# Two neighbouring PSUM banks for every step that takes two, in a kernel whose order a planner makes

## The chip, the core and the metric

The kernel runs on one core of a Trainium2 chip. The metric is the time of one execution in microseconds, as the device counts it; the number to predict is the median of several executions. The core has five engines with a queue each: TensorE (PE in the profile, with its weight loads shown apart as PEld), VectorE (DVE), ScalarE (ACT), GpSimd (POOL) and SyncE (SP, which here issues DMAs). Every queue is worked off in the order in which the program wrote it. An instruction that depends on another engine's work waits at a semaphore, and everything behind it in its own queue waits with it. PE leaves its results in PSUM, 128 partitions of eight banks with 512 f32 values each; VectorE and ScalarE read them there.

## What is computed

Two stages follow each other. The first is a Nystrom attention over 8 batches, 8 heads, 576 positions and a head size of 64, with 32 landmarks: three softmaxes, a pseudo-inverse by six iterations, and a product of four factors.

```
A = sm(q, k_lm);  Bm = sm(q_lm, k_lm);  C = sm(q_lm, k)     # k_lm, q_lm: means of 18 positions
Z = Bm.T / (norm_1(Bm) * norm_inf(Bm) + 1e-06)
for _ in range(6):
    Z = 2 * Z - Z @ Bm @ Z
x = A @ Z @ C @ v
```

The second is a mixture of 8 experts over the 4608 resulting rows of 512 values. Each row goes to the expert with the largest logit, and is scaled by that expert's gate.

```
logits = normalize(x) @ normalize(expert_emb).T / tau
e = argmax(logits);  out = gate[e] * (relu(x @ w1[e]) @ w2[e])       # w1: 512x1024, w2: 1024x512
```

## The kernel before

The kernel guesses one expert for each batch, runs the whole batch through it, and has a general path (the function `general`) for inputs in which a row chose otherwise; on the inputs timed here that path is not taken. f32 factors are split into two f16 parts, so a product takes three f16 matmuls.

Each batch is cut into steps, written as Python generators. `inverse` forms the landmark softmax; `powers` does the six iterations (tile `ek`); `values` is C times v in two halves (tiles `ec`, `ct`, `u`); `queries` is A in two halves (transposed into `ae`, then `ab`); `landmarks` forms the combined factor and the logits' weights (`wgd`); `rows` gives logits and norms in five chunks (its last reader is ScalarE's `junk`, L1134); `first_weights` folds the attention factor into w1 (`ww`), and `first` and `second` are the expert's two layers (`ht`, `yt`). `first` and `second` are the bulk of PE's work. The other steps of the batches to come are woven into it.

What sets the order is the class `Weave`, a planner that runs on the host while the program is written. Each generator yields what it wants next: an engine for so many nanoseconds (`T`, `V`, `A`, `G`), a buffer (`get`), or a flag. The planner keeps a clock for each engine, takes the request that can start first, or among those close to it the one of highest priority, and lets that generator write its instructions. So the instructions of every queue stand in the order in which the planner started them. A buffer carries the planned time at which it came free, and whoever asks gets the ones that have been free longest.

PSUM is one tile `ps` of eight banks (L489). A step calls `take(n)` for one or two banks. Shares limit how many banks a kind of step may hold: 5 for attention steps, 3 for the first layer, 2 for the second. One bank, the highest, is kept for matmuls that only keep the array busy (`keep_warm`, L598) until the first expert layer starts, and joins the others then. Two banks at once are taken by `inverse` (1 time a batch), `values` (4), `queries` (2), `landmarks` (1), `rows` (5) and `first_weights` (4), which is 17 takes for each of eight batches, 136 in all. If the two banks that came free first are x and y, the step's view of them is `ps[:, x:y + 1:y - x]`: a slice that starts at bank x and steps by y - x.

No wait is written by hand. The framework that records the instructions compares what each of them reads and writes and places the semaphore waits. In the built program of this kernel, 282 waits between PE, DVE and ACT join two instructions that have no bank in common, and no other tile either; in each of the 282 one side holds a pair of banks that are apart, and the other side's bank lies between them. The planner knows nothing of such waits.

Of the kernel before, what the change touches and what calls it, by code (L numbers as in the profile page):

```python
# [60 lines left out]
GUESS_LAT = 2500.0  # L61
NBANKS = 8
NSUM = 3

ATT, NPH, NPY = 5, 3, 2

# [41 lines left out]
class Weave:  # L108
# [64 lines left out]
    def tally(self, name, n):  # L173

        self.count[name] += 1
        if self.count[name] == n:
            self.flag(name)

    def _start(self, g, safe=True):
        r, t = g[3], g[1]  # L180
        if r[:2] == ("use", "pe") and safe:
            m = self.margin if g[5] else self.bmargin
            return max(t, g[6] + m, self.free["pe"])
        if r[0] == "use":
            return max(t, self.free[r[1]])
        if r[0] == "sleep":
            return t + r[1]
        if r[0] == "until":
            return max(t, r[1])
        if r[0] == "any":  # L190
            return min(max(t, self.free[o[0]]) for o in r[1])
        if r[0] == "get":
            b, n = self.buffers[r[1]], r[3] if len(r) > 3 else 1
            return max(t, sorted(b)[n - 1][0]) if len(b) >= n else None
        return max(t, self.flags[r[1]]) if r[1] in self.flags else None

    def run(self, *until):

        while self.gens and not (until and all(f in self.flags for f in until)):
            ready = [(self._start(g), g) for g in self.gens]  # L200
            ready = [(t, g) for t, g in ready if t is not None]

            safe = min((t for t, g in ready if g[3][:2] == ("use", "pe")), default=0.0)
            if safe > self.free["pe"]:
                ready = [(min(t, self._start(g, False)) if g[3][:2] == ("use", "pe") else t, g) for t, g in ready]
            assert ready, [g[3] for g in self.gens]
            first, lead = min(ready, key=lambda x: (x[0], x[1][3][0] in ("use", "any")))
            at, best = max(((t, g) for t, g in ready if g[3][:2] == lead[3][:2] and t <= first + SLACK),
                           key=lambda x: (x[1][3][2] if x[1][3][0] == "get" and len(x[1][3]) > 2 and x[1][3][2] is not None else x[1][2], -x[0]))
            r = best[3]  # L210
            if r[0] == "use":

                soon = [(t, g) for t, g in ready if g[2] >= max(AHEAD, best[2] + 100) and g[3][:2] == r[:2] and t < at + r[2] - EPS]
                if soon:
                    at, best = min(soon, key=lambda x: x[0])
                    r = best[3]
            g_t, best[1], best[4] = best[1], at, None
            if r[0] == "any":
                t = g_t
                r = ("use", *min(r[1], key=lambda o: max(t, self.free[o[0]]) + sum(o[1:]))[:2])  # L220
                best[4] = r[1]
                at = max(t, self.free[r[1]])
            if r[:2] == ("use", "pe") and self.warm:
                t = self.free["pe"]
                ns = self.warm((at - t) * (0.5 if self.cold(t) else 1.0) * WARM if at - t > WMIN else 0.0)
                if ns:
                    self.array(t, ns, 2.3 * ns)
                ns = self.warm(self.lacking(at))
                if ns:
                    at = self.array(at, ns, 2.3 * ns)  # L230
            self.last = at
            if r[0] == "use":
                end = self.array(at, r[2], r[4]) if r[1] == "pe" else at + r[2]
                self.free[r[1]] = end
                best[1] = end + (LAT[r[1]] if r[3:4] in ((), (None,)) else r[3])

                best[6] = best[1] if best[1] > end else 0.0
            elif r[0] == "get":
                got = sorted(self.buffers[r[1]])[:r[3] if len(r) > 3 else 1]
                best[6] = max(best[6], got[-1][0])  # L240
                for x in got:
                    self.buffers[r[1]].remove(x)
                best[4] = [i for _, i in got]
            elif r[0] == "wait":
                best[6] = max(best[6], self.flags[r[1]])
            self._step(best)
        self.now = self.last
# [228 lines left out]
def nystrom_moe(ctx: ExitStack, tc: tile.TileContext, qT, kT, v, emb, w1, w2, out):  # L476
# [12 lines left out]
    ps = psum.tile([P, NBANKS, 512], F32, name="ps")  # L489

    def view(ids):

        if len(ids) == 1:
            return ps[:, ids[0]]
        x, y = sorted(ids)
        return ps[:, x:y + 1:y - x]

    def take(n, share="att"):

        yield "get", share, None, n  # L500
        ids = yield "get", "bank", None, n

        def done():
            wv.put("bank", *ids)
            wv.put(share, *ids)

        return view(ids), done
# [158 lines left out]
    def sums(b, nm, src):  # L666
        if b >= NSUM:
            yield "wait", ("a", b - NSUM)
            yield "wait", ("u", b - NSUM)
        sm = sums_of[nm, b] = wk.tile([P, 4, M], F32, name=nm + "sum", bufs=NSUM)  # L670
        half = None
        for x in range(2):
            r = 2 * x
            yield "wait", (nm, b, x)
            if b == 1:
                yield "wait", ("e", 0)
            sv = src[:, r:r + 2].rearrange("p r (m t) -> p (r m) t", t=SEG)
            if (yield "any", (("pool", 1360), ("dve", 1270, SBIAS if b >= SUMS_DVE else -SBIAS))) == "pool":
                yield "get", "half"
                half = wk.tile([P, 2 * M, SEG // 2], F32, name="half", bufs=1)  # L680
                pool.tensor_tensor(out=half, in0=sv[:, :, 0:9], in1=sv[:, :, 9:18], op=ALU.add)  # L681
                yield V(576)
                sv = half
            vec.tensor_reduce(sm[:, r:r + 2].rearrange("p r m -> p (r m)"), sv, axis=AX.X, op=ALU.add)
            if sv is half:
                wv.put("half")
        wv.flag((nm + "s", b))
        wv.tally((nm + "use", b), 3)
# [786 lines left out]
    n = nc.values_load(mi[0:1, 0:1], min_val=0, max_val=NT)  # L1475
# [41 lines left out]
```

## Time and profile before

| | |
|---|---|
| median of three executions | 544.4 us (542.37 to 549.75) |
| the profiled execution, its own time | 546.0 us |
| its span, from the first to the last instruction | 544.3 us |
| mean granted TensorE clock | 0.976 of full speed |
| busy: PE, DVE, ACT, POOL | 459.4, 350.3, 248.3, 81.7 us |
| instructions on PE, DVE, ACT | 5664, 1123, 576 |

Busy time is the time in which an engine had an instruction in work; the rest of the span it stood idle. The view of waits adds up, for pairs of engine and tile, the idle time that ended when the second finished; it says how often this happened and what the longest stop was. The timeline shows instructions in the order of time, with the idle time before each and who ended it in brackets. The windows view gives the busy time of each engine in a stretch of the span, and the clock granted there (PEclk).

### The profile page before, as it was taken

To read this page: it belongs to the slowest core of one execution; us is meant where nothing else is said; L and a number is where in the kernel's file an instruction comes from. 1 tells how busy PE (TensorE), PEld (TensorE's weight loads), DVE (VectorE), ACT (ScalarE), POOL (GpSimd) and SP (SyncE) were. 2 spreads that over 40 slices of the span, in tenths; PEclk is the share of its full clock that TensorE was granted. 3 is DMA by queue.
4 is the path that set the end of the run, shared out by engine and by line. 5 is a ranking of instruction groups with operands and counts; after the bars stand their busy time and mean duration, and the time that the engine had idled before them with its cause. 6 is when DMAs were issued, how large, how long until landed. Compare 5 with 4: busy or idle time off the path is not lost. (4 is left out here: it accounts for less than half of the span.)

```text
span 544.3 us, 13967 instructions
## 1 busy us (share of the span) xinstructions
PE 459.4 (84%) x5664; PEld 251.3 (46%) x5664; DVE 350.3 (64%) x1123; ACT 248.3 (46%) x576; POOL 81.7 (15%) x79
## 2 busy tenths in 40 slices
PE   8797897898787878977999988888878779989994
PEld 3343553435543344532555445543545336635642
DVE  5696794679777675686875728878454766654400
ACT  1266333653466323673358315854157333852410
POOL 2054000023100310233301000322000000010000
PEclk9799898999999998899999999999999999999998
DMA  8693226562159412952258015801172011821011
GB/s 315 236 374 101 88 90 238 162 227 89 45 185 319 160 52 61 375 178 107 85 206 331 35 55 171 325 22 63 60 261 95 20 40 43 308 84 48 3 58 36
DMA packets 29945, 78.22 MB, mean 144 GB/s; under 512 B 2864, under 2 KB 14256, under 8 KB 28080
## 3 DMA queue, kind: packets, MB, share of 16 engines
q1 hardware_dynamic: 29728, 77.15, 39.5%
q8 instruction: 46, 0.75, 0.6%
q14 instruction: 27, 0.22, 0.1%
q10 hardware_dynamic: 144, 0.10, 0.1%
HBM read 61.96 MB, written 15.27 MB: 142 GB/s over the span
## 5 line engine op out<-in xcount | busy, mean ns | idle before, releaser
L510 PE MATMUL ps<-w2c,ht 128*128 128x512 f16 (+1 forms) x1152 | 211.1, 346 | 22.2 <-DVE ww L1297 6.2
L510 PEld LDWEIGHTS <-ht 128*128 128x128 f16 (+1 forms) x1152 | 90.3, 102 | 109.8 <-issue 43.7
L510 PE MATMUL ps<-ab,ww 128*128 128x288 f16 x768 | 112.8, 291 | 15.9 <-DVE ae L872 3.2
L510 PEld LDWEIGHTS <-ww 128*128 128x128 f16 x768 | 71.9, 99 | 50.2 <-issue 26.1
L1343 ACT ACTIVATE ht<-ps 128x288 f16<-128x288 f32 x128 | 51.9, 408 | 57.0 <-PE ps L510 41.7
L1345 DVE SCALAR_TENSOR_TENSOR ht<-ps,ht 128x288 f16<-128x288 f32 x128 | 56.7, 449 | 30.1 <-ACT ht L1343 22.7
L1421 ACT ACTIVATE yt<-ps,gfac 128x512 f32<-128x512 f32 (+1 forms) x34 | 21.8, 642 | 66.7 <-PE ps L510 50.6
L1335 DVE SCALAR_TENSOR_TENSOR w2c<-wstage,wsc,w2c 128x1024 f16<-128x1024 f32 x32 | 41.8, 1307 | 0.2
L1134 ACT ACTIVATE junk<-ps 128x512 bf16<-128x512 f32 (+1 forms) x40 | 23.9, 596 | 38.1 <-PE ps L510 15.3
L1297 DVE SCALAR_TENSOR_TENSOR ww<-ps,wsc,ww 128x512 f16<-128x512 f32 x32 | 23.8, 745 | 25.0 <-PE ps L510 15.5
L1308 ACT ACTIVATE junk<-wstage 128x1024 bf16<-128x1024 f32 x32 | 33.8, 1057 | 6.5 <-DMA wstage<-w 6.2
L1295 ACT ACTIVATE ww<-ps,wsc 128x512 f16<-128x512 f32 x32 | 22.0, 687 | 28.6 <-PE ps L510 27.4
L1331 DVE TENSOR_SCALAR w2c<-wstage,wsc 128x1024 f16<-128x1024 f32 x30 | 23.0, 767 | 18.3 <-PE ps L510 18.3
L1267 ACT ACTIVATE junk<-wstage 128x1024 bf16<-128x1024 f32 x32 | 33.7, 1054 | 1.3 <-DMA wstage<-w 1.2
L681 POOL TENSOR_TENSOR half<-k_t 128x576 f32<-128x576 f32 x14 | 20.8, 1488 | 68.1 <-DMA k_t<-kT 38.3
L904 POOL TENSOR_TENSOR ae<-ae,am 128x576 f32<-128x576 f32 x9 | 10.8, 1205 | 127.1 <-DVE am L877 109.6
L510 PE MATMUL ps<-ek 32*32 32x64 f32 (+1 forms) x768 | 20.3, 219 | 7.6 <-DVE ae L872 1.9
L598 PE MATMUL ps<-ones 128*128 128x512 bf16 (+3 forms) x97 | 24.3, 399 | 2.3 <-POOL ones L535 2.3
L510 PE MATMUL ps<-wstage,wt 64*32 64x256 f32 x512 | 22.2, 388 | 3.3 <-ACT junk L1134 1.9
L681 POOL TENSOR_TENSOR half<-q_t 128x576 f32<-128x576 f32 x14 | 19.6, 1397 | 35.0 <-DMA q_t<-qT 22.4
L510 PE MATMUL ps<-wgd,ab 64*128 64x136 f16 (+1 forms) x480 | 21.1, 222 | 3.8 <-ACT ww L1295 2.2
L510 PEld LDWEIGHTS ps<-ek 32*32 32x32 f32 x768 | 12.6, 105 | 23.3 <-issue 8.3
(175 smaller groups left out, 558.3 us busy)
## 6 DMA issues: line engine op xcount, KB each, us to landing
wstage<-w SPq DMA_DIRECT2D x64, 512.0 KB, 7.1
v_t<-v SPq DMA_DIRECT2D x16, 512.0 KB, 8.5
out<-yt SPq DMA_DIRECT2D x32, 256.0 KB, 2.0
k_t<-kT SPq DMA_DIRECT2D x7, 1152.0 KB, 7.4
q_t<-qT SPq DMA_DIRECT2D x7, 1152.0 KB, 9.3
abs__133<-ab SPq DMA_DIRECT2D x8, 576.0 KB, 3.3
k_t<-kT SPq DMA_DIRECT2D x2, 576.0 KB, 4.5
q_t<-qT SPq DMA_DIRECT2D x2, 576.0 KB, 6.5
```

What stands on the lines that cost most here:

```text
L510: pe.matmul(o, lhsT, rhs, start=start, stop=stop)
L598: pe.matmul(warmth[:, 0:k * P], ones16, bc(ones16.unsqueeze(1), [P, k, P]), start=True, stop=True)
L681: pool.tensor_tensor(out=half, in0=sv[:, :, 0:9], in1=sv[:, :, 9:18], op=ALU.add)
L1134: act.activation(junk[lo:hi, 0:512].rearrange("p (i g x) -> p i g x", i=2, g=2), pfv[:, :, :, 0:2 * D], AF.Square, accum_out=ssq[lo:hi, cg ...
L1267: act.activation(junk, stage[1, b, q], AF.Square, accum_out=sq[:, q:q + 1])
L1295: act.activation(ww[:, 0], pww, AF.Copy, scale=sc)
L1297: vec.scalar_tensor_tensor(out=ww[:, 1], in0=pww, scalar=sc, in1=ww[:, 0], op0=ALU.mult, op1=ALU.subtract)
L1308: act.activation(junk, stage[2, b, q], AF.Abs, accum_out=sq[:, q:q + 1])
L1331: vec.tensor_scalar(w[:, 0], st, sc, None, op0=ALU.mult)
L1335: vec.scalar_tensor_tensor(out=w[:, 1], in0=st, scalar=sc, in1=w[:, 0], op0=ALU.mult, op1=ALU.subtract)
L1343: act.activation(ht[:, 0, r], ph[:, 0:HS], AF.Relu)
L1345: vec.scalar_tensor_tensor(out=ht[:, 1, r], in0=ph[:, 0:HS], scalar=0.0, in1=ht[:, 0, r], op0=ALU.max, op1=ALU.subtract)
```

## The change

Steps that take two banks now get two neighbours: among all free neighbouring pairs, the one whose later bank came free earliest. A step that takes one bank gets the one with the smallest value of its planned free time plus 2000 ns for each neighbour that is on the free list too. The view of two banks becomes a plain slice. Buffers other than banks are given out as before.

```diff
+ALONE = 2000.0
...
+    def _pick(self, name, _=None, n=1):
+
+        b = self.buffers[name]
+        if name != "bank":
+            return sorted(b)[:n] if len(b) >= n else None
+        at = {i: t for t, i in b}
+        if n == 2:
+            pairs = [(max(at[i], at[i + 1]), i) for i in at if i + 1 in at]
+            return [(at[i], i) for i in range(min(pairs)[1], min(pairs)[1] + 2)] if pairs else None
+        return [min(b, key=lambda x: (x[0] + sum(ALONE for i in (x[1] - 1, x[1] + 1) if i in at), x[1]))] if b else None
...
         if r[0] == "get":
-            b, n = self.buffers[r[1]], r[3] if len(r) > 3 else 1
-            return max(t, sorted(b)[n - 1][0]) if len(b) >= n else None
+            got = self._pick(*r[1:])
+            return max(t, max(got)[0]) if got else None
...
-                got = sorted(self.buffers[r[1]])[:r[3] if len(r) > 3 else 1]
-                best[6] = max(best[6], got[-1][0])
+                got = self._pick(*r[1:])
+                best[6] = max(best[6], max(got)[0])
...
     def view(ids):
-        if len(ids) == 1:
-            return ps[:, ids[0]]
-        x, y = sorted(ids)
-        return ps[:, x:y + 1:y - x]
+        return ps[:, ids[0]] if len(ids) == 1 else ps[:, ids[0]:ids[0] + 2]
```

The instructions stay the same in kind and number but for the ones whose engine the planner chooses when it places them: three elementwise operations on `ae` go from POOL to DVE, one on `bbd` from DVE to POOL, and two copies of `ek` from ACT to DVE. None of the 282 waits described above is left in the built program. The order changes on all engines from the first expert layer on; before that it is the same. Two places show what becomes of it. After the change all lines from L510 on have numbers higher by ten.

The first place is on PE in `landmarks` of the second batch: after a group of the second expert layer (`w2c`, `ht`) PE multiplies the batch's `u` by the result `ek` of the iterations. Before the change:

```order
L510 LDWEIGHTS ht_962
L510 MATMUL ps_74<-w2c_1057,ht_962 128x512
L510 MATMUL ps_74<-u_156,ek_1162 32x64 [waits Activation_49]
L510 MATMUL ps_74<-u_156,ek_1162 32x64 x7
L510 MATMUL ps_74<-bbd1_125,u_156 64x64 x4
```

And the same place after the change:

```order
L520 LDWEIGHTS ht_962
L520 MATMUL ps_74<-w2c_1056,ht_962 128x512
L520 MATMUL ps_74<-u_156,ek_1162 32x64 [waits DVE_49]
L520 MATMUL ps_74<-u_156,ek_1162 32x64 x7
L520 MATMUL ps_74<-bbd1_125,u_156 64x64 [waits Pool_49]
L520 MATMUL ps_74<-bbd1_125,u_156 64x64 x3
```

The matmuls stand in the same order; the first on `u` and `ek` waited for ACT's reader of a pair of banks and now waits for DVE, for the instruction that writes `ek_1162`, and the next product waits for `bbd1`, which POOL now makes.

The second place is on DVE in `queries` of the fourth batch, where the scores leave PSUM for `ae` (L872 before, L882 after). Before the change:

```order
L810 TENSOR_REDUCE cm_2995<-ps_74 128x1 [waits PE_49]
L963 TENSOR_TENSOR ek_3005<-ps_74,ek_2870 128x64 [waits Activation_49]
L812 TENSOR_SCALAR cm_2995<-cm_2995 128x1 [waits DVE_49]
L872 STREAM_TRANSPOSE ae_3030<-ps_74 128x576 [waits Activation_49]
L790 TENSOR_SCALAR cs_3028<-cs_3028 128x1
L877 TENSOR_REDUCE am_3032<-ae_3030 128x18 [waits DVE_49]
```

The same step after the change:

```order
L1341 TENSOR_SCALAR w2c_2665<-wstage_2397,wsc2_2506 128x1024 [waits DMAHW6_49,PE_49]
L882 STREAM_TRANSPOSE ae_2677<-ps_74 128x576 [waits PE_49]
L1345 SCALAR_TENSOR_TENSOR w2c_2665<-wstage_2397,wsc2_2506,w2c_2665 128x1024 [waits DVE_49]
L947 TENSOR_SCALAR whb_2684<-ps_74 128x1 [waits PE_49]
L887 TENSOR_REDUCE am_2679<-ae_2677 128x18 [waits DVE_49]
L951 TENSOR_SCALAR invw_117<-whb_2684 128x1 [waits DVE_49]
L882 STREAM_TRANSPOSE ae_2688<-ps_74 128x576
```

The transpose waited for ACT and now waits for PE, whose matmuls fill its own two banks; and a second transpose of a `queries` half follows five rows later, where the two halves of a batch stood farther apart before.

## The prediction, made before the run

> **What bounds the kernel now.** I read the page's busy shares first, then the view of PE's waits, then timelines around the longest of them, and last a table by stretches.
>
> ```profile
> PE 459.4 (84%) x5664; PEld 251.3 (46%) x5664; DVE 350.3 (64%) x1123; ACT 248.3 (46%) x576; POOL 81.7 (15%) x79
> ```
>
> PE is the busiest engine by far, and its matmuls run to the end of the span. So the kernel's time is PE's work plus PE's idle time, 544.3 - 459.4 = 84.9 us. The view of PE's waits says who ended that idle time (engine and line, the one waited for; us in total, times, longest).
>
> ```profile
> PE ps L510 <- ACT junk L1134: 14.5, 15, 2.3
> PE ps L510 <- ACT ww L1295: 9.7, 13, 1.0
> PE ps L510 <- DVE ww L1297: 8.8, 11, 1.4
> PE ps L510 <- DVE ae L872: 7.0, 7, 1.4
> PE ps L510 <- DVE cm L810: 5.9, 8, 1.2
> PE ps L510 <- ACT ec L817: 4.7, 7, 1.9
> PE ps L510 <- DVE be L712: 4.0, 5, 1.9
> PE ps L510 <- DVE lg L1132: 3.5, 10, 0.6
> PE ps L823 <- ACT ec L817: 2.8, 3, 0.9
> PE ps L823 <- DVE cm L810: 2.5, 2, 1.9
> PE ps L510 <- DVE ht L1345: 1.4, 2, 0.8
> ```
>
> The first ten rows sum to 63.4 us, and all ten are readers of a two-bank view. The reader of the expert's single banks, the last row, cost 1.4 us. PE is not short of data; it stands behind whoever empties a pair of banks. At the first place of the order it looks like this:
>
> ```profile
> 79.42 0.21 DVE L963 TENSOR_TENSOR ek<-ps,ek 128x64 f32<-128x64 f32 x1
> 80.39 0.82 PE L510 MATMUL ps<-w2c,ht 128*128 128x512 f16 x3
> 81.78 0.60 ACT L1134 ACTIVATE junk<-ps 128x512 bf16<-128x512 f32 x1 [2.97 <-DVE lg L1132]
> 82.72 0.60 ACT L1134 ACTIVATE junk<-ps 128x512 bf16<-128x512 f32 x1 [0.26 <-DVE lg L1132]
> 83.47 0.43 PE L510 MATMUL ps<-u,ek 32*32 32x64 f32 x16 [2.26 <-ACT junk L1134]
> ```
>
> PE needs `ek`, which DVE finished at 79.42 + 0.21 = 79.63, and is free at 81.21. It starts at 83.47, when ACT's second `junk` reader is done. That reader holds banks 1 and 6 in the program, PE's product goes to bank 2. These are 2.26 us for nothing. The second place shows a row of them:
>
> ```profile
> 215.31 0.91 PE L510 MATMUL ps<-ab,ww 128*128 128x288 f16 x6
> 216.26 0.74 ACT L817 ACTIVATE ec<-ps,cm 128x576 f32<-128x576 f32 x1 [1.47 <-PE ps L510]
> 217.12 0.78 DVE L872 STREAM_TRANSPOSE ae<-ps 128x576 f32<-128x576 f32 x1 [2.02 <-ACT ec L817]
> 217.96 0.65 PE L510 MATMUL ps<-ek 32*32 32x64 f32 x16 [1.74 <-DVE cs L790]
> ```
>
> ACT's `ec` (banks 2 and 7) waits for an expert matmul in bank 5; DVE's `ae` (0 and 4) waits for that `ec`; PE's product into bank 1 waits for that `ae` (the row names `cs`, which ends at nearly the same time). Three engines take turns where each had its own banks.
>
> **The change part by part.** *The waits that go.* By the program, none of these links is left. How much of the 63.4 us goes? Not all of it was for nothing: some stops were for a bank that PE really wanted. Taking each of PE's stops behind a reader without a common bank, and counting only the time after everything else it needed was done, I come to some 57 us; an estimate, from matching the trace with the program. Nor does a removed stop shorten the kernel by itself, because the next true wait may take it up. So I size the gain by how densely PE runs here where such stops are few (us, then busy time of PE, PEld, DVE, ACT and POOL, PEclk, DMA share, GB/s):
>
> ```profile
> 0.00:27.20 27.20, 21.03 (x246) 10.42 (x250) 15.82 (x63) 4.99 (x12) 5.08 (x18) 0.87 0.75 276
> 81.60:108.90 27.30, 21.75 (x330) 10.76 (x331) 14.41 (x75) 14.00 (x36) 1.18 (x1) 0.94 0.59 200
> 217.70:244.90 27.20, 22.92 (x369) 12.58 (x370) 21.59 (x61) 19.35 (x43) 6.82 (x6) 0.94 0.79 276
> 272.10:299.40 27.30, 25.05 (x403) 15.73 (x402) 16.93 (x74) 19.13 (x48) 3.18 (x3) 1.00 0.74 268
> 299.40:326.60 27.20, 25.31 (x226) 12.32 (x225) 13.53 (x47) 7.84 (x19) 1.18 (x1) 1.00 0.12 45
> 489.90:517.10 27.20, 26.37 (x214) 17.32 (x214) 13.37 (x29) 9.10 (x20) 0.00 (x0) 1.00 0.08 25
> 517.10:544.30 27.20, 19.17 (x125) 9.78 (x122) 0.48 (x1) 2.75 (x4) 0.00 (x0) 0.90 0.14 47
> ```
>
> Between 272 and 327 us, with attention steps woven in, PE is busy for 25.05 of 27.30 and 25.31 of 27.20 us, 92 and 93%; at 490 to 517, 97%. Between 27.2 and 517.1 us PE has 459.4 - 21.03 - 19.17 = 419.2 us of work in 489.9 us, 86%. At 93% this body takes 450.8 us, a gain of 39.1; at 97%, 432.2 us, a gain of 57.7. I take 93%, because the other stretches hold as much attention work as these two and none as little as the last.
>
> *The head.* Up to 27.2 us the first batch is a chain of dependent steps, and the array is kept busy with filler. A few of the stops lie in it, such as this one:
>
> ```profile
> 25.84 0.43 PE L510 MATMUL ps<-ek 32*32 32x64 f32 x16 [1.04 <-DVE ae L872]
> ```
>
> I take 2 us, with bounds of 0 and the 6.2 us that PE idles there.
>
> *The clock.* After the first 27 us there are four stretches of 3.4 us in which the granted clock was half:
>
> ```profile
> 61.00:64.40 3.40, 3.34 (x15) 2.30 (x15) 2.23 (x10) 0.68 (x3) 1.22 (x1) 0.50 0.37 155
> 84.90:88.30 3.40, 3.40 (x20) 1.31 (x15) 0.59 (x5) 1.38 (x5) 0.81 (x1) 0.50 0.98 380
> 204.30:207.70 3.40, 3.40 (x43) 1.69 (x42) 1.40 (x6) 0.92 (x4) 0.00 (x0) 0.51 0.00 0
> 218.00:221.40 3.40, 3.40 (x62) 2.14 (x62) 1.71 (x5) 1.19 (x3) 1.16 (x1) 0.50 1.00 341
> ```
>
> Each costs 3.4 / 2 = 1.7 us of PE, 6.8 in all. Two of them start right behind the two places shown (83.47 and 217.96), so I let those two go: 3.4 us. The bounds are 6.8 gained, and 3.4 lost if the new order brings two more. The Trainium skill's page "TensorE: Matmul & The Clock Gate" (Part 1: The HAM clock gate) says that the clock halves after an idle window of about 3.4 us; this trace halves it with no PE wait above 2.3 us. By the page's figure these stops could not have caused the halvings, and the term would be 0; the measurement decides.
>
> *What moves or stays.* A few small operations change engines, and pairs are read at another distance. The rows of both, the last one with smallest, median and largest duration:
>
> ```profile
> L906 DVE TENSOR_TENSOR ae<-ae,am 128x576 f32<-128x576 f32 x7 | 5.5, 790 | 0.0
> L961 DVE COPY ek<-ps 128x64 f32<-128x64 f32 x18 | 4.0, 220 | 7.8 <-PE ps L510 5.8 <-ACT junk L1134 2.0
> L971 DVE TENSOR_TENSOR bbd<-ek,block 128x256 f32<-128x256 f32 x1 | 0.4, 407 | 0.0
> L1134 ACT ACTIVATE junk<-ps x40: 587/597/625, 77.8 to 482.0; 128x512 bf16<-128x512 f32 x32, 64x512 bf16<-64x512 f32 x8
> ```
>
> The same matmuls are issued, so PE's work stays. Three `ae` operations more on DVE, one `bbd` fewer and two `ek` copies more are 3 x 0.79 - 0.41 + 2 x 0.22 = 2.4 us on an engine that has 350 us of work in 544; I cost them at nothing, hidden by PE. Should one of the three land in front of a PE wait, it costs its 0.8 us. Reading two neighbours instead of banks apart is worth nothing: `junk` read pairs from one to seven banks apart, and its forty instructions lie between 587 and 625 ns. The tail has single banks only: 0.
>
> *Sum:* 39.1 + 2 + 3.4 = 44.5 us. The profiled execution's own time is 546.0, so 501.5 for such a run; it was 1.6 us above the median of 544.4, and by that median the forecast is 499.9, say 500 us.
>
> **The rivals.** *True waits take up half of it.* With PE faster, DVE has less time for the same work. In the stretch at 217.70 DVE is busy for 21.59 us; were it cut to 22.92 / 0.93 = 24.6 us, DVE would be at 88% and its own chains would show. For it: DVE's 350 us would be 70% of 500. Against: ACT and DVE lose waits of the same kind (the `ec` and `ae` rows above), so they come earlier too. Half of 39.1 and the other terms at half, 22 us: 522 us.
>
> *PE would have waited anyway.* Each stop ends at a reader, and the next true wait on the same chain would stop PE as long. The first place speaks against it: what PE needed there had been ready for 3.8 us. At most 5 us would be left: 540 us, within 2%.
>
> *The new choice of banks costs more than the waits did.* So far a bank was given out that had been free longest. Now a pair must be neighbours, and a single bank may be one just freed, so a matmul may stand right behind the true reader of its own bank; and steps are bunched, as the two `queries` halves are at the second place. Priced by the mean stop in the `junk` row, 14.5 / 15 = 1.0 us: if 0.6 us fell on each of the 136 two-bank takes, 82 us would come against 57 that go, 569 us. It decides from 57 / 136 = 0.42 us a take, and is measurably slower from 0.5. Against it: in the written order, the cases in which a bank is filled within six matmuls of its last reader's place fall from 40 of 556 to 30, so reuse isn't closer on the whole. The Trainium skill speaks for this rival: its page "Perfetto Trace Analysis" (Optimizing Tensor Performance, Matmuls) has matmul groups rotate through the banks so that emptying one overlaps the next group. By that rule a narrower choice would lengthen the time, toward the 569 us above.
>
> **How the numbers follow.** A run of this kernel can be told from no change from 2% on, that is below 533.5 or above 555.3 us. The forecast, with PE between 90 and 97% dense in the body, gets 0.62; the half gain 0.19; no effect 0.12; the slower rival 0.07. The forecast's own range is 482 to 515 (97% with 6 us from the head and clock is 544.4 - 57.7 - 6 = 481; 90% is a body of 465.8, a gain of 24.1, and 5.4 from head and clock, 515). Reaching over the half gain as well, with 8 us of room for the head and the clock behind it, the range is 482 to 531, and leaves out the last two cases, 0.19. Faster by over 2% is 0.62 + 0.19 and a little of the third, 0.82; the same 0.11; slower 0.07.
>
> **What would show it.** If I am right, PE's waits for `junk`, `ww`, `ae`, `cm` and `ec` fall from 63.4 us to under 25; PE's busy share rises above 90%; the windows from 27 us to the tail show 93% on average; and the half-clock stretch behind `landmarks` of the second batch is gone. At that place PE's `u,ek` matmul starts right behind the group of `w2c`. I am wrong if those rows keep their size, now with readers of the very bank that PE fills, or if DVE fills up beyond 90% in several stretches while PE's idle time remains. The step most open is the density of 93%, taken from two stretches.

## The result, and the profile after

The changed kernel takes 473.7 us in the median (472.5 to 477.4), against 545.7 us (542.4 to 549.8) for the kernel before beside it: a ratio of 0.869, with a 95% interval of 0.861 to 0.877. It is faster, as forecast, but by 72 us where 44 were forecast, and the time lies 8 us below the range. The profiled execution took 472.5 us, with a span of 470.7 us.

The page's busy shares of the changed kernel:

```profile
PE 444.9 (95%) x5664; PEld 249.0 (53%) x5664; DVE 350.8 (75%) x1127; ACT 245.2 (52%) x574; POOL 80.4 (17%) x77
```

PE's idle time fell from 84.9 to 470.7 - 444.9 = 25.8 us, by 59.1. PE's busy time fell too, from 459.4 to 444.9 us, by 14.5, with the same matmuls. The two make up the 73.6 us by which the span shrank. DVE and ACT have nearly the same work as before in a shorter span.

The view of PE's waits of the changed kernel, its six longest (line numbers are higher by ten):

```profile
PE ps L520 <- DVE ht L1355: 2.9, 3, 1.6
PE ps L520 <- ACT junk L1144: 2.5, 4, 1.3
PE ps L608 <- POOL ones L545: 2.3, 1, 2.3
PE ps L520 <- DVE ww L1307: 2.0, 4, 0.9
PE ps L520 <- DVE gfac L1218: 1.7, 1, 1.7
PE ps L520 <- DVE scw L1029: 1.2, 1, 1.2
```

The readers of two-bank views that ended 63.4 us of idle time before are down to `junk` with 2.5, `ww` with 2.0 and a few below: `ec` 1.0, `be` 0.6, `ae` 0.5. At the first place of the order, the timeline of the changed kernel now reads:

```profile
67.32 0.21 DVE L973 TENSOR_TENSOR ek<-ps,ek 128x64 f32<-128x64 f32 x1
68.48 0.82 PE L520 MATMUL ps<-w2c,ht 128*128 128x512 f16 x3
69.23 0.43 PE L520 MATMUL ps<-u,ek 32*32 32x64 f32 x16
69.59 0.45 PE L520 MATMUL ps<-bbd,u 128*64 128x64 f32 x8
69.97 0.39 PE L520 MATMUL ps<-w2c,ht 128*128 128x512 f16 x1
```

PE goes from the expert's group to `u,ek` with no idle time, where it stood for 2.26 us; the row of `bbd` shows that the wait for POOL costs nothing either. The body of the span, before and after, in the windows view (us, busy time of PE, PEld, DVE, ACT, POOL, clock, DMA share, GB/s), first of the kernel before:

```profile
27.20:517.10 489.90, 419.19 (x5307) 231.06 (x5300) 334.02 (x1060) 240.56 (x560) 76.63 (x61) 0.99 0.40 142
```

and of the changed kernel, with four stretches of it below:

```profile
27.20:443.50 416.30, 401.95 (x5205) 227.53 (x5206) 329.87 (x1051) 235.61 (x553) 74.11 (x58) 0.98 0.46 164
...
81.60:108.90 27.30, 27.13 (x460) 13.51 (x459) 24.74 (x65) 16.34 (x38) 7.89 (x5) 1.00 0.67 231
163.30:190.50 27.20, 23.30 (x303) 13.64 (x303) 25.20 (x80) 14.56 (x37) 6.57 (x5) 0.87 0.37 125
244.90:272.10 27.20, 26.52 (x316) 13.12 (x313) 26.44 (x81) 16.35 (x42) 12.37 (x10) 1.00 0.58 214
326.60:353.80 27.20, 27.20 (x429) 16.58 (x426) 22.83 (x68) 17.52 (x41) 1.16 (x1) 1.00 0.48 171
```

The body's density went from 86% to 401.95 / 416.3 = 97%. Three of the four stretches shown are full of attention steps and have next to no idle time on PE, with DVE busy for 84 to 97% of them. The one at 163.3 us is the least dense of the body, 86%: DVE is busy for 93% of it. It holds the second place of the order, where the two `queries` halves now stand close together. PE's stops there are of 0.48, 0.57 and 1.19 us, and each ends at an instruction of DVE:

```profile
163.80 0.67 PE L520 MATMUL ps<-wstage,wt 64*32 64x256 f32 x16 [0.48 <-DVE ae L882]
165.03 0.22 PE L520 MATMUL ps<-wgd,ab 64*128 64x136 f16 x1 [0.57 <-DVE whb L947]
166.44 0.51 PE L520 MATMUL ps<-wgd,ab 64*128 64x136 f16 x11 [1.19 <-DVE scw L1029]
```

So the waits on other banks are gone at this place too, and what stands in their stead is a DVE that is busy without a break from 163.7 to 167.1 us.

### The profile page after: what moved, and what is told of

It is laid out like the page before. It is cut to its first block, busy times and chain, and to the rows that moved or that the text cites. A ratio compares the mean times of both kernels' runs of the same rounds, so it can differ in the third digit from the quotient of the medians.

```text
span 470.7 us, 13962 instructions
## 1 busy us (share of the span) xinstructions
PE 444.9 (95%) x5664; PEld 249.0 (53%) x5664; DVE 350.8 (75%) x1127; ACT 245.2 (52%) x574; POOL 80.4 (17%) x77
## 5 line engine op out<-in xcount | busy, mean ns | idle before, releaser
L520 PE MATMUL ps<-w2c,ht 128*128 128x512 f16 (+1 forms) x1152 | 205.5, 345 | 1.7 <-DVE gfac L1218 1.7
L520 PE MATMUL ps<-ab,ww 128*128 128x288 f16 x768 | 111.5, 292 | 3.0 <-DVE ht L1355 2.9
L1355 DVE SCALAR_TENSOR_TENSOR ht<-ps,ht 128x288 f16<-128x288 f32 x128 | 56.4, 451 | 19.2 <-ACT ht L1353 18.7
L1431 ACT ACTIVATE yt<-ps,gfac 128x512 f32<-128x512 f32 (+1 forms) x34 | 21.8, 642 | 61.8 <-PE ps L520 57.8
L1341 DVE TENSOR_SCALAR w2c<-wstage,wsc 128x1024 f16<-128x1024 f32 x30 | 24.6, 820 | 6.9 <-PE ps L520 6.8
L691 POOL TENSOR_TENSOR half<-q_t 128x576 f32<-128x576 f32 x14 | 21.3, 1521 | 13.7 <-DMA q_t<-qT 4.8
L914 POOL TENSOR_TENSOR ae<-ae,am 128x576 f32<-128x576 f32 x7 | 8.1, 1157 | 87.6 <-DVE am L887 81.5
L520 PEld LDWEIGHTS <-ab 64*128 64x128 f16 (+1 forms) x480 | 15.1, 98 | 12.1 <-issue 11.2
```

The costliest lines, as they stand in the source:

```text
L520: pe.matmul(o, lhsT, rhs, start=start, stop=stop)
L1341: vec.tensor_scalar(w[:, 0], st, sc, None, op0=ALU.mult)
L1355: vec.scalar_tensor_tensor(out=ht[:, 1, r], in0=ph[:, 0:HS], scalar=0.0, in1=ht[:, 0, r], op0=ALU.max, op1=ALU.subtract)
```

## The experiments

Two theories. A: the waits on a tile in another bank are the whole effect, and the new order is neutral. B: the forecast was right for the waits, some 45 us, and the rest comes from the new order and choice of banks. The planner's order and the physical banks can be changed apart from each other, which tells them apart both ways. In the table, "foreign waits" are those that join two instructions without a common bank, counted in the built program (in brackets those on PE); stops are PE's idle times over 50 ns, counted in the trace; the last column is PE's busy time less half of what lies in stretches of half clock. Each ratio is to the kernel before timed beside that run, which took between 543 and 546 us in the median; where two runs are close, the ratios compare better than the times.

| run | us, median | ratio, 95% | foreign waits | PE stops | idle in them, us | PE busy, us | without the clock's share |
|---|---|---|---|---|---|---|---|
| before | 545.7 | | 282 (102) | 98 | 76.9 | 459.4 | 449.7 |
| changed kernel | 473.7 | 0.869 (0.861 to 0.877) | 0 | 30 | 18.1 | 444.9 | 439.1 |
| e1_apart | 547.4 | 1.005 (1.002 to 1.009) | 320 (121) | 96 | 77.3 | 462.5 | 448.1 |
| e2_old_order | 476.4 | 0.875 (0.870 to 0.881) | 0 | 29 | 21.1 | 446.3 | 441.8 |
| e3_two_apart | 494.5 | 0.908 (0.901 to 0.914) | 148 (60) | 52 | 38.1 | 446.5 | 442.6 |
| e4_no_alone | 473.2 | 0.870 (0.865 to 0.875) | 0 | 25 | 23.1 | 441.6 | 438.1 |
| e5_old_order_spread | 475.6 | 0.874 (0.869 to 0.878) | 0 | 23 | 21.1 | 445.5 | 439.4 |
| e6_margin_300 | 477.0 | 0.877 (0.874 to 0.881) | 0 | 32 | 23.5 | 445.1 | 440.5 |
| e7_margin_1000 | 476.2 | 0.877 (0.875 to 0.880) | 0 | 26 | 21.8 | 443.4 | 437.9 |
| e8_three_apart | 508.6 | 0.937 (0.933 to 0.940) | 209 (78) | 59 | 45.1 | 453.4 | 444.7 |

**The new order with the old waits.** The changed kernel's planner runs as it is; only the view lays its banks elsewhere.

```diff
+PLACE = [0, 4, 1, 5, 2, 6, 3, 7]
...
     def view(ids):
-        return ps[:, ids[0]] if len(ids) == 1 else ps[:, ids[0]:ids[0] + 2]
+        ids = [PLACE[i] for i in ids]
+        if len(ids) == 1:
+            return ps[:, ids[0]]
+        x, y = sorted(ids)
+        return ps[:, x:y + 1:y - x]
```

> The changed kernel with its planner, its order and its choice of banks untouched; only the planner's bank i is laid in another physical bank (0, 4, 1, 5, 2, 6, 3, 7), so that each pair is 3 or 4 banks apart again and is seen through a stepped slice. Every engine's order is that of the changed kernel, instruction for instruction; 320 waits on a tile in another bank come back (282 in the kernel before). Theory A, the waits are the whole effect: 545 us or a little more, PE idle 75 to 90 us, PE busy near 459 us. Theory B, the new order brings the part of the gain that was not forecast (some 27 of 72 us): about 515 to 520 us.

It took 547.4 us, all of the gain given back, with PE idle for 84.9 us. Its busy shares look like those of the kernel before:

```profile
PE 462.5 (84%) x5664; PEld 253.4 (46%) x5664; DVE 353.1 (64%) x1127; ACT 248.5 (45%) x574; POOL 78.9 (14%) x77
```

so do the longest of its PE waits (lines are six higher than in the changed kernel):

```profile
PE ps L526 <- DVE ww L1313: 16.8, 18, 2.7
PE ps L526 <- ACT junk L1150: 11.2, 12, 2.0
PE ps L526 <- ACT ww L1311: 9.4, 12, 1.1
PE ps L526 <- DVE ae L888: 6.2, 7, 1.3
PE ps L526 <- DVE cm L826: 6.2, 6, 2.0
```

and in its timeline the first place has its stop again:

```profile
83.20 0.43 PE L526 MATMUL ps<-u,ek 32*32 32x64 f32 x16 [2.02 <-ACT junk L1150]
```

Theory B falls: with the waits in it, the changed kernel's order brings none of the 27 us. The layout has 38 foreign waits more than the kernel before, so a gain of a few microseconds from the order could hide behind them; the next run bounds it.

Nor is it the stepped slice as such that costs the time. ACT's `junk`, which reads a pair, takes 597 ns in the median with pairs apart (the kernel before and this run) and with neighbours:

```profile
L1144 ACT ACTIVATE junk<-ps x40: 580/597/606, 65.9 to 393.4; 128x512 bf16<-128x512 f32 x32, 64x512 bf16<-64x512 f32 x8
```

**The old order without the waits.** The kernel before keeps its planner and its order; where its planner names banks, a list made beforehand says which neighbours are used in their place.

```diff
+BANKS = ("...428 digits, one for each take")
...
-        return view(ids), done
+        first = int(BANKS[taken["n"]])
+        taken["n"] += 1
+        return view([first, first + 1][:n]), done
```

> The kernel before with its planner untouched; the banks are given out by a list made beforehand, in which every pair is two neighbours. Every engine's order is that of the kernel before, instruction for instruction, and no wait on a tile in another bank is left. Theory A: 470 to 480 us, as the changed kernel. Theory B: about 500 us, as forecast for the waits alone. A third reading, that the planner's rule for neighbours costs some order: under 470 us.

Its busy shares:

```profile
PE 446.3 (94%) x5664; PEld 248.7 (52%) x5664; DVE 345.8 (73%) x1123; ACT 247.0 (52%) x576; POOL 82.4 (17%) x79
```

476.4 us: the old order, instruction for instruction, gains what the changed kernel gains, within 3 us, and the intervals of the two ratios overlap. With the run before, the cause is shown from both sides: it is the waits, and neither the order nor the planner's rule for neighbours adds anything that these runs can tell.

**How the loss grows.** Two more layouts of the changed kernel's banks give fewer foreign waits, by `PLACE` of 0, 2, 4, 6, 7, 5, 3, 1 and of 0, 3, 1, 4, 2, 5, 7, 6.

> As the run with pairs apart, but the planner's banks laid as 0, 2, 4, 6, 7, 5, 3, 1, so that pairs are at most two apart with one bank between; 148 waits on a tile in another bank, order as in the changed kernel. Theory A: the cost goes with the number of such waits, 474 + 148/320 of the loss with pairs apart: 505 to 512 us. Theory B: 490 to 497 us. If it is the stops of PE that also lengthen its busy time, by some 0.19 us a stop (459.4 - 444.9 us less 1.7 us of clock, over 98 - 30 stops), PE is busy for about 452 us here.

> As the run e3_two_apart, with the planner's banks laid as 0, 3, 1, 4, 2, 5, 7, 6: pairs are two or three apart, 209 waits on a tile in another bank, 78 of them on PE. Order as in the changed kernel. So far 0, 148 and 320 such waits gave 473.7, 494.5 and 547.4 us. If the cost goes with their number, a line between the last two gives 513 us; if it goes with how many banks lie in between, a step nearer to the run with pairs 3 and 4 apart, 525 to 540 us. PE's busy time without the clock's share (half of the busy time in half-clock stretches) is 439.1, 442.6 and 448.1 us at 30, 52 and 96 stops: if each stop adds to it, it lies between 443 and 447 us here.

494.5 and 508.6 us. With 0, 148, 209 and 320 foreign waits the loss is 0, 21, 35 and 74 us. So more waits cost more, but the cost of one rises, from 0.14 to 0.17 and 0.23 us. The first run came out faster than a proportional loss (505 to 512), inside the range that its expectation gave for theory B; as theory B has fallen with the first two runs, what this refutes is the proportional cost. Its forecast for PE's busy time, made with 0.19 us a stop, missed too: 446.5 us for some 452. The second run came out a little under the line between its neighbours (513) and not near the run with pairs farther apart, and without the clock's share PE was busy for 444.7 us, inside the 443 to 447 of its expectation. Whether a wait across more banks is dearer, or whether waits on three engines add up to chains as at the second place of the order, these runs don't separate; the number and the distance change together.

**The planner's price for a lone bank.** `ALONE = 0.0` in the changed kernel.

> The changed kernel with the 2000 ns for a free neighbour set to 0: single banks go out longest free first, as before the change, pairs are still neighbours. The order changes; no wait on a tile in another bank. Theory A: 470 to 480 us. If the choice of single banks matters for how soon pairs are free, 480 to 490 us.

473.2 us: the second half of the change, by which single banks go first where both neighbours are in use, makes no difference that can be told.

**Quick reuse of banks.** The old order once more, with another list of neighbours.

> The order of the kernel before and neighbouring pairs, as in the run e2_old_order (476.4 us), with another list of banks. There, 355 of 564 banks were given out within 300 ns of coming free on the planner's clock (245 in the kernel before, which takes the longest free first); here 267. No wait on a tile in another bank in either. If quick reuse of a bank costs time, as the third rival and the rule of rotating through the banks have it, this run is faster than 476.4 us by the stops behind readers of the bank that PE fills, up to 5 us: 471 to 474 us. If it doesn't, 475 to 478 us.

475.6 us against 476.4, with intervals of the ratio that overlap for the most part. How soon a bank is given out again cost nothing that can be measured, in the span between 267 and 355 quick reuses of 564. Both lists use all eight banks, so a much narrower choice wasn't tried.

**The planner's margins.** `MARGIN` and `BMARGIN` of the changed kernel at 300 and 200, and at 1000 and 700.

> The changed kernel, with the planner's margin for PE (the time by which it prefers a matmul's inputs to be ready ahead) cut from 600 to 300 ns, and that of the bulk from 400 to 200. The order changes. If PE's remaining 18 us of stops come from a margin that is too small for the chip, this is slower, 478 to 490 us. If the margin had served to soften the waits that are gone now, it is as fast or faster: 468 to 474 us.

> As the run before it in this list, the other way: margins of 1000 and 700 ns. If the remaining stops come from a margin that is too small, PE's stops fall below 18 us and the time to 465 to 472 us. If not, 472 to 480 us.

477.0 and 476.2 us, neither below 473.7; the ratios are 0.877 for both, at the upper end of the changed kernel's interval. The smaller margin is 1 us short of the "slower" that its expectation named, with 23.5 us of stops; the larger didn't bring PE's stops down either (21.8 us, against 18.1). So neither direction of the margin helps. What the remaining stops hang on isn't settled by these runs, since the order changes with the margin. No version tried here beats the changed kernel by more than the measurement can tell.

## Why the prediction fell short

The forecast was 39.1 us in the body, 2 in the head and 3.4 of clock, 44.5 in all. Of the 73.6 us by which the span shrank, PE's idle time gave 56.4 in the body (from 70.7 to 14.3), 2.4 in the head and 0.4 in the tail, the clock 3.9, and the rest of PE's busy time 10.6.

**Right: what goes and why.** PE stood behind readers of pairs that held none of the banks it wanted; these stops are gone, at the place named and in sum (63.4 us to about 7), and the run with the old order shows that nothing else was needed. My estimate of some 57 us for them is close to the 58.8 us by which PE's stops shrank (76.9 to 18.1). That reading two neighbours instead of banks apart is worth nothing was right as well, by the row of `junk` above.

**Wrong: the density of 93%.** The step "I take 93%, because the other stretches hold as much attention work as these two" sized the body's gain at 39.1 us. The body measured 97%, and 56.4 us. The two stretches that I took as the model weren't free of such stops, they only had fewer: of the 4.1 us that PE idled in them, the view of waits puts some 3.2 us down to readers of pairs. The changed kernel's stretches at 81.6 and 326.6 us reach 99 and 100%. I had 57 us on the table, from the stops themselves, and discounted it by a third, for true waits that would take their place. They took up little: the 22 us of the one rival on that side and the 5 us of the other are both far from 72. DVE, at 75% of the whole, mostly kept up; it lost 95 foreign waits of its own, which is the reason that the prediction itself gave against the rival. But the rival's mechanism is there in small. DVE is busy for over 90% of five of the body's stretches of 27 us, and in two of them PE idles for 2.7 and 3.9 us; and of PE's remaining stops some 11.7 us end at DVE.

**Wrong: "the same matmuls are issued, so PE's work stays".** Their number stays, but PE's busy time fell by 14.5 us. Of this 3.9 us are clock: PE's busy time inside half-clock stretches fell from 19.3 to 11.6 us, half of which is extra. The other 10.6 us come with the stops. It could be read in the timeline of before, where groups of 6, 12 and 18 equal matmuls stand:

```profile
71.27 0.91 PE L510 MATMUL ps<-ab,ww 128*128 128x288 f16 x6
65.60 1.65 PE L510 MATMUL ps<-ab,ww 128*128 128x288 f16 x12
73.11 2.38 PE L510 MATMUL ps<-ab,ww 128*128 128x288 f16 x18
```

They stand in the order of their size. Six more take 0.74 and 0.73 us; the first six take 0.91. So 0.17 us of a group is the run-out of its last matmul, which the next group covers if it follows at once, and which is paid where PE stops. 68 stops fewer at 0.17 us are 11.6 us, against 10.6 measured. Taken stop by stop, the last matmul outlasts the usual step to the next of its kind by 0.20 us in the mean in both traces: 17.9 us at 91 stops before, 4.9 us at 25 after (for the other stops the step can't be read). All ten profiles go the same way: the last column of the table is 437.9 to 441.8 us at 23 to 32 stops, 442.6 and 444.7 at 52 and 59, and 448.1 and 449.7 at 96 and 98, some 0.14 us a stop. The run with 59 stops was forecast by this reading, at 443 to 447 us; the earlier one for the run with 52 stops, made with 0.19 us a stop, came out too high. That each stop pays a run-out wasn't tried by itself, and the ends of matmuls are modelled in this profile; the fit is what speaks for it, so the cause of the 10.6 us is argued and not shown. This term, taken as 0, is what put the time below the range: the low end of 482 us already held a body at 97%.

**Right in size by luck: the clock.** 3.4 us were forecast, for two of the four stretches behind the head, and 3.9 measured over the whole span. Behind the head only 1.0 us of it was gained: PE's busy time in half-clock stretches there fell from 13.5 to 11.6 us. The stretch behind `landmarks` of the second batch is gone, as named. The other one that I let go is not: the changed kernel has a half-clock stretch right behind the second place, from 167.1 us on, twice as long as before, and one more of 6.8 us at 112.5. The rest, 2.9 us, comes from the stretch in the head, 16.6 to 23.4 us, which the forecast didn't count. This compares one profiled execution of each kernel.

**The head.** PE's idle time up to 27.2 us fell from 6.2 to 27.2 - 23.41 = 3.8 us, 2.4 for the 2 forecast. The windows view of the changed kernel:

```profile
0.00:27.20 27.20, 23.41 (x342) 11.46 (x346) 20.41 (x76) 6.85 (x17) 6.26 (x19) 1.00 0.88 320
```

**The slower rival.** The choice of banks that costs more than the waits did: refuted in the price it rested on. It needed 0.42 us for each of the 136 two-bank takes to cancel the gain; the readers of pairs now end under 7 us of PE's idle time in all, 0.05 us a take. That bunched `queries` halves can cost something is seen at the second place, 2.2 us. The rule of the Trainium skill's page "Perfetto Trace Analysis" (Optimizing Tensor Performance, Matmuls), to rotate through the banks, showed no effect where it was tried: 476.4 us with quick reuse, 475.6 us with less of it.

## What to carry to other kernels

When one engine is the bound and its idle time is spent behind readers, ask of each long wait whether the two instructions share anything; a stepped slice over a tile can make the recorded accesses cover what lies between, and then every engine waits for strangers. If nothing is shared, take the stops at their full length first and let a rival show that something else would fill them, since the other engines lose such waits too. And count the stops as well as their time: in these profiles PE's busy time falls by about 0.14 us with each one that goes.

## What was not expected of the hardware

The granted clock halved without any long stop of PE. In the windows view, the 3.4 us ahead of the four half-clock stretches after the head of the kernel before:

```profile
57.60:61.00 3.40, 2.12 (x21) 1.08 (x18) 2.63 (x11) 1.74 (x4) 0.00 (x0) 1.00 0.63 197
81.50:84.90 3.40, 1.44 (x44) 1.17 (x46) 1.04 (x5) 1.89 (x7) 0.00 (x0) 1.00 0.36 69
200.90:204.30 3.40, 1.49 (x14) 1.13 (x12) 3.20 (x14) 1.70 (x4) 0.00 (x0) 1.00 0.09 20
214.60:218.00 3.40, 1.57 (x18) 0.73 (x21) 1.16 (x5) 1.32 (x4) 0.00 (x0) 1.00 0.74 204
```

and ahead of the two of the changed kernel, with one of them:

```profile
109.10:112.50 3.40, 1.62 (x21) 1.14 (x21) 3.40 (x8) 0.41 (x1) 1.25 (x1) 1.00 0.60 215
112.50:119.30 6.80, 5.95 (x43) 3.20 (x42) 4.20 (x9) 2.50 (x7) 1.75 (x2) 0.50 0.00 1
163.70:167.10 3.40, 1.39 (x28) 0.70 (x28) 3.40 (x9) 0.88 (x2) 1.16 (x1) 1.00 0.48 104
```

In five of the six PE was busy for 1.39 to 1.62 of 3.4 us, 41 to 48%, while its longest stop after its first matmul was 2.3 us in the one kernel and 1.7 us in the other; the sixth had 62%. In both of the changed kernel's stretches DVE was busy for the whole 3.40 us. The Trainium skill's page "TensorE: Matmul & The Clock Gate" (Part 1: The HAM clock gate) speaks of an idle window; here a half-idle one was enough, most of the time. All drops of a profile lie on one grid of 3.41 us, to within 0.05 us. Over all ten profiles, 29 of the 31 drops ahead of PE's last matmul follow a stretch of 3.4 us in which PE was busy for 6 to 52%, the other two 60 and 63%; eleven stretches of the same grid at 44 to 52% were not followed by one. So the busy share alone doesn't decide it; what else does is open.
